# Attention and feed-forward on one core: 17-row score matmuls, an immediate exp bias, fuller PV groups, a reordered VectorE chain and a prologue without GpSimd fills

## The chip, the cores and the metric

The kernel runs on one core of one Trainium2 chip. The metric is the device time of one execution in microseconds (us); lower is better. Executions of one kernel are timed several times, beside executions of the kernel before on the same chip. A run is called slow when it lies over 1.5% above the fastest run of the same kernel; ratios use the others.

"Clock" always means the mean granted TensorE clock, as a share of full speed. It is a column of the profile.

## The reference

```python
def _A_ref(x, wqkv, wo):               # x [1, 2048, 512], H = 32 heads of Dh = 16
    q, k, v = split((x @ wqkv), 3, heads)
    scores = einsum("bhqd,bhkd->bhqk", q, k) * (Dh ** -0.5)
    p = softmax(scores)
    return merge(einsum("bhqk,bhkd->bhqd", p, v)) @ wo

def _B_ref(x, w1, w3, w2):             # F = 1792
    return (silu(x @ w1) * (x @ w3)) @ w2

xn = layernorm(x)
out = x + _A_ref(xn, wqkv, wo) + _B_ref(xn, w1, w3, w2)
```

This is abridged. Both blocks read the same normalized x, so the feed-forward work can fill TensorE's gaps in the attention. What matters here: 32 heads of only 16 dimensions, 2048 x 2048 scores for each head, all exponentiated.

## The kernel before

**The planner.** The order of the instructions on every engine is fixed when the kernel is built. A greedy planner simulates the engines with assumed costs (`dur=`), and at each step gives TensorE the first thing that can go: a score pair for ScalarE ("A"), a score pair for VectorE ("D"), a PV group, or a piece of a dense tile (K, Q, V, feed-forward, output).

**Scores.** Each of 1024 score pairs is two matmuls of 32 rows (the contraction) and 512 columns, on two of the four 32-row groups of the array; in the trace the two start 3 ns apart and are over in 0.39 us (medians at full clock). Only 16 rows are head dimensions. Row 16 of K and Q holds constants whose product adds a bias to each score. Rows 17 to 31 are zero. So the whole of KT and QT must be filled before K and Q are copied in, by ScalarE and GpSimd.

```python
def score(b0, name, dur):
    ...
    for i in range(2):
        j = j0 + i
        mms.append((b0 + i, KT[32 * j:32 * j + 32, g, kt * 128:(kt + 1) * 128],
                    QT[32 * j:32 * j + 32, u % 4, :], 32 * j))
    ...                                        # matmul(bank(b), l_, r_, tile_position=(rp, 0))

for g in range(2, NG):                         # prologue: six of these on GpSimd
    P.post("pool", lambda g=g: ... e.tensor_scalar(KT[:, g, :],
        sel1[:, 0:1].to_broadcast((128, S)), YB, None, ALU.mult) ..., ready=9.0 + g, prio=3)
```

**Exponentials.** ScalarE takes 798 of the pairs, with the bias in an SBUF column. VectorE takes 226, as a chain of five operations: clip to 16 bits (`yb`), mantissa (`mb`), exponent (`e`), correction (`g`), product (`t`).

```python
q = P.op("act", lambda e: e.activation(PT[:, s_, :], ps[:, b0 * 512:(b0 + 2) * 512], ACTF.Exp,
                                       scale=ASC, bias=act_bias[:, 0:1]), ..., dur=a_cost(1024))
...
for f_ in (f_m, f_e, f_g, f_t):                # e, g, t also write the shared keys XD
    P.post("dve", f_, ready=0.0, prio=2)
P.post("dve", p1, ready=o.end + _LAT, prio=3, cond=lambda: bool(slot()))
```

**PV.** Up to four matmuls of 128 rows and 17 columns stand side by side in the four 32-column groups, one for each of four heads, and run together: at 602.35 us of the trace four are over in 0.39 us, and one alone takes 0.38. A group that isn't full waits at most 1.2 us of planned time for its fellows.

```python
if len(pick) < 4 and not closed and P.t - oldest < 1.2:
    return False
...
ins = e.matmul(bank(PV)[32 * j:32 * j + 17, :], v_, p_, ..., tile_position=(0, 32 * j))
```

Dense tiles are cut the same way: four 32-column matmuls of 128 rows side by side.

## Time and profile before

| | before |
|---|---|
| time, median of the runs beside the change | 969.09 us (966.78 to 971.25) |
| prologue, 0 to 75 us | ScalarE 28.5 us busy, TensorE 44.1 |
| steady, 500 to 700 us | ScalarE 99%, VectorE 96%, TensorE 94% busy, clock 1.00 |
| tail, after the last exp | 43 us |

These lines are from the page of the kernel before: the span, the busy time of each engine (share of the span, number of instructions), the busy tenths and the clock tenths in 40 slices of the span, and the chain that ended last, by engine.

```profile
span 968.4 us, 21733 instructions
PE 858.6 (89%) x9033; PEld 240.4 (25%) x9033; DVE 878.7 (91%) x1437; ACT 853.9 (88%) x872; POOL 91.4 (9%) x82
...
PE   4669888989888999998989999999999999999985
...
DVE  7969797999899999999999999999999999999951
ACT  3339798999899999999999999999999999999930
...
PEclk9779799999989999999999999999999999999988
...
ACT 43%; DVE 33%; PE 17%; issue 2%; DMA 2%; SPq 2%; DVEq 0%
```

Three engines are near full for most of the span, and the chain lies mostly on the two that exponentiate. ScalarE is busy for only three tenths of the first three slices. Next, four groups of instructions: line, engine, operation, tiles, shapes and count; then busy us and mean ns of one; then the idle time before them and what ended it.

```profile
L1550 ACT ACTIVATE f_PT<-ps,f_act_bias 128x1024 bf16<-128x1024 f32 x798 | 819.1, 1153 | 51.3 <-PE ps L1513 44.1
L1513 PE MATMUL ps<-f_QT,f_KT 32*128 32x512 bf16 x2048 | 330.4, 391 | 42.4 <-ACT f_PT L1550 23.7
...
L1134 DVE TENSOR_SCALAR f_xn_sb<-f_xd,f_lnr,f_lnb 128x512 bf16<-128x512 bf16 x16 | 35.3, 2244 | 0.3 <-POOL f_lnb L1122 0.3
```

One of the 16 layer-norm scalings takes 2244 ns on average. The timelines of VectorE and of GpSimd show what the long ones run beside (start us, us, instruction):

```profile
26.82 10.83 DVE L1134 TENSOR_SCALAR f_xn_sb<-f_xd,f_lnr,f_lnb 128x512 bf16<-128x512 bf16 x2
```

```profile
26.77 10.73 POOL L1158 TENSOR_SCALAR f_KT<-f_sel 128x2048 bf16<-128x2048 f32 x2
```

Two scalings last as long as two GpSimd fills, within 0.1 us; two that run beside no fill, at 25.58 us, take 0.72 us. Last, the table of stretches: stretch, length, busy us (count) of PE, PEld, DVE, ACT and POOL, then the clock, the DMA share and GB/s.

```profile
0.00:75.00 75.00, 44.13 (x482) 17.00 (x482) 62.41 (x76) 28.51 (x32) 49.78 (x51) 0.84 0.37 100
75.00:300.00 225.00, 197.28 (x1898) 51.29 (x1890) 202.72 (x335) 204.93 (x208) 9.33 (x7) 0.94 0.23 31
500.00:700.00 200.00, 187.73 (x1994) 51.21 (x1994) 192.00 (x326) 198.51 (x204) 9.45 (x7) 1.00 0.25 29
927.00:968.00 41.00, 28.50 (x467) 12.35 (x463) 12.00 (x24) 1.79 (x3) 0.00 (x0) 0.86 0.21 37
```

### The profile page before, as it was taken

To read this page: it belongs to the slowest core of one execution; us is meant where nothing else is said; L and a number is where in the kernel's file an instruction comes from. 1 tells how busy PE (TensorE), PEld (TensorE's weight loads), DVE (VectorE), ACT (ScalarE), POOL (GpSimd) and SP (SyncE) were. 2 spreads that over 40 slices of the span, in tenths; PEclk is the share of its full clock that TensorE was granted. 3 is DMA by queue.
4 is the path that set the end of the run, shared out by engine and by line. 5 is a ranking of instruction groups with operands and counts; after the bars stand their busy time and mean duration, and the time that the engine had idled before them with its cause. 6 is when DMAs were issued, how large, how long until landed. Compare 5 with 4: busy or idle time off the path is not lost.

```text
span 968.4 us, 21733 instructions
## 1 busy us (share of the span) xinstructions
PE 858.6 (89%) x9033; PEld 240.4 (25%) x9033; DVE 878.7 (91%) x1437; ACT 853.9 (88%) x872; POOL 91.4 (9%) x82
## 2 busy tenths in 40 slices
PE   4669888989888999998989999999999999999985
PEld 2222122222222222222222222222222222222232
DVE  7969797999899999999999999999999999999951
ACT  3339798999899999999999999999999999999930
POOL 7840000000000000000000000000000000000000
PEclk9779799999989999999999999999999999999988
DMA  4501221312311222303232222222231212233221
GB/s 154 136 16 28 37 39 23 50 22 27 51 13 13 24 19 24 46 17 41 29 45 34 18 25 24 45 34 36 28 45 21 29 18 23 34 46 40 35 36 37
DMA packets 90685, 35.34 MB, mean 36 GB/s; under 512 B 74448, under 2 KB 88528, under 8 KB 90576
## 3 DMA queue, kind: packets, MB, share of 16 engines
q1 hardware_dynamic: 90576, 33.85, 24.7%
q8 instruction: 73, 1.20, 0.5%
q14 instruction: 36, 0.29, 0.1%
HBM read 22.81 MB, written 2.10 MB: 26 GB/s over the span
## 4 chain that ended last, share of the span: by engine, by line
ACT 43%; DVE 33%; PE 17%; issue 2%; DMA 2%; SPq 2%; DVEq 0%
ACT f_PT L1550 42%; DVE f_yb L1593 9%; PE ps L1216 8%; PE ps L1513 5%; DVE f_xd L1627 4%; PE ps L1673 4%; DVE f_xd L1610 3%; DVE f_xd L1621 3%; DVE f_mb L1616 3%; DVE f_xn_sb L1134 3%; DVE f_t L1350 2%; ACT f_th L1346 2%; SPq L1283 1%; DVE f_hT L1360 1%; DMA f_wkv<-in_A_wqkv_dram 1%
## 5 line engine op out<-in xcount | busy, mean ns | idle before, releaser
L1550 ACT ACTIVATE f_PT<-ps,f_act_bias 128x1024 bf16<-128x1024 f32 x798 | 819.1, 1153 | 51.3 <-PE ps L1513 44.1
L1513 PE MATMUL ps<-f_QT,f_KT 32*128 32x512 bf16 x2048 | 330.4, 391 | 42.4 <-ACT f_PT L1550 23.7
L1593 DVE TENSOR_SCALAR f_yb<-ps 128x1024 int16<-128x1024 f32 x226 | 274.4, 1214 | 5.3 <-PE ps L1513 4.9
L1673 PE MATMUL ps<-f_PT,f_Vaug 128*17 128x512 bf16 x1596 | 240.5, 389 | 4.5 <-DVE f_xd L1610 3.8
L1673 PE MATMUL ps<-f_xd,f_Vaug 128*17 128x512 bf16 x1356 | 238.7, 388 | 4.5 <-DVE f_xd L1610 2.9
L1216 PE MATMUL ps<-f_xnT,f_w 128*32 128x512 bf16 x1792 | 169.7, 396 | 19.4 <-DVE f_t L1350 13.8
L1513 PEld LDWEIGHTS ps<-f_QT,f_KT 32*128 32x128 bf16 x2048 | 83.0, 91 | 374.3 <-ACT f_PT L1550 291.8
L1627 DVE TENSOR_TENSOR f_xd<-f_yb,f_mb 128x1024 bf16<-128x1024 bf16 x226 | 159.5, 706 | 8.9
L1726 POOL TENSOR_TENSOR f_onorm<-f_U,f_R 128x512 bf16<-128x512 f32 x31 | 41.6, 1343 | 812.1 <-DMA f_R<-f_Rrow 532.3
L1616 DVE TENSOR_SCALAR f_mb<-f_yb 128x1024 int16<-128x1024 int16 x226 | 100.8, 446 | 5.1
L1621 DVE TENSOR_SCALAR f_xd<-f_yb 128x1024 int16<-128x1024 int16 x226 | 98.9, 438 | 7.1
L1610 DVE TENSOR_SCALAR f_xd<-f_yb 128x1024 int16<-128x1024 int16 x226 | 101.3, 448 | 0.0
L1673 PEld LDWEIGHTS ps<-f_PT,f_Vaug 128*17 128x17 bf16 x1596 | 55.4, 88 | 109.6 <-issue 83.0
L1216 PE MATMUL ps<-f_w,f_hT 128*32 128x512 bf16 x896 | 75.8, 381 | 0.5 <-DVE f_hT L1360 0.5
L1673 PEld LDWEIGHTS ps<-f_xd,f_Vaug 128*17 128x17 bf16 x1356 | 57.1, 89 | 69.6 <-issue 29.3
L1216 PEld LDWEIGHTS ps<-f_xnT,f_w 128*32 128x32 bf16 x1792 | 45.6, 96 | 70.2 <-issue 54.1
L1216 PE MATMUL ps<-f_wo,f_onorm 128*32 128x512 bf16 x512 | 46.0, 381 | 0.2 <-DVE f_wkv L1400 0.2
L1350 DVE SCALAR_TENSOR_TENSOR f_t<-f_th,ps 128x512 bf16<-128x512 f32 x56 | 38.1, 680 | 7.4 <-ACT f_th L1346 6.8
L1346 ACT ACTIVATE f_th<-ps 128x512 f32<-128x512 f32 x56 | 35.2, 629 | 10.6 <-PE ps L1216 10.6
L1360 DVE SCALAR_TENSOR_TENSOR f_hT<-f_t,ps 128x512 bf16<-128x512 bf16 x56 | 38.1, 681 | 4.1 <-PE ps L1216 2.6
L1134 DVE TENSOR_SCALAR f_xn_sb<-f_xd,f_lnr,f_lnb 128x512 bf16<-128x512 bf16 x16 | 35.3, 2244 | 0.3 <-POOL f_lnb L1122 0.3
L1216 PE MATMUL ps<-f_wkv,f_xnT 128*32 128x512 bf16 x256 | 24.4, 488 | 11.6 <-DVE f_t L1350 7.5
(54 smaller groups left out, 276.7 us busy)
## 6 DMA issues: line engine op xcount, KB each, us to landing
f_w<-in_B_w_dram SPq DMA_DIRECT2D x112, 128.0 KB, 2.8
f_R<-f_Rrow SPq DMA_DIRECT2D x128, 32.0 KB, 4.0
f_KT<-f_stg SPq DMA_DIRECT2D x128, 16.0 KB, 1.8
f_QT<-f_stg SPq DMA_DIRECT2D x128, 16.0 KB, 1.8
f_xr<-in_A_x_dram SPq DMA_DIRECT2D x16, 128.0 KB, 2.2
out_dram<-f_xn_sb SPq DMA_DIRECT2D x16, 128.0 KB, 1.9
f_w<-in_B_w_dram SPq DMA_DIRECT2D x1, 1792.0 KB
f_xd<-in_A_x_dram SPq DMA_DIRECT2D x3, 512.0 KB
```

Of the source, the lines that this page charges most:

```text
L1134: o = P.op("dve", lambda e: e.tensor_scalar(xn_sb[:, xs, :], x_sb[:, t, :], lnr[:, t:t + 1], lnb[:, t:t + 1], ALU.mult, ALU.add), reads=[( ...
L1216: ins = e.matmul(bank(bk)[32 * i:32 * i + 32, 0:ncols], make_lhsT(i), rhs_ap, start=start, stop=stop, tile_position=(0, 32 * i))
L1346: q = P.op("act", lambda e: e.activation(th[:, ss, :], bank(bk), ACTF.Tanh, scale=0.5), reads=[("ps", bk)], writes=[("th", ss)], dur=a_cos ...
L1350: q2 = P.op("dve", lambda e: e.scalar_tensor_tensor(t1[:, ss, :], th[:, ss, :], 1.0, bank(bk), ALU.add, ALU.mult), reads=[("th", ss), ("ps ...
L1513: ins = e.matmul(bank(b), l_, r_, start=True, stop=True, tile_position=(rp, 0))
L1550: q = P.op("act", lambda e: e.activation(PT[:, s_, :], ps[:, b0 * 512:(b0 + 2) * 512], ACTF.Exp, scale=ASC, bias=act_bias[:, 0:1]), reads= ...
L1593: q = P.op("dve", lambda e: e.tensor_scalar(yb[:, ys, :], ps[:, 4 * 512:6 * 512], 0.0, 32767.0, ALU.max, ALU.min), reads=[("ps", 4), ("ps" ...
L1610: q_ = P.op("dve", lambda e: e.tensor_scalar(dsl[:, s_, 0, :], yb[:, ys, :], 0x7F80, None, ALU.bitwise_and), reads=[("yb", ys)], writes=[( ...
L1616: P.op("dve", lambda e: e.tensor_scalar(mb[:, ys, :], yb[:, ys, :], 0x7F, 0x3F00, ALU.bitwise_and, ALU.bitwise_or), reads=[("yb", ys)], wr ...
L1621: q_ = P.op("dve", lambda e: e.tensor_scalar(dsl[:, s_, 1, :], yb[:, ys, :], -352.0, 0.0, ALU.add, ALU.max), reads=[("yb", ys)], writes=[( ...
L1627: q_ = P.op("dve", lambda e: e.tensor_tensor(dsl[:, s_, 2, :].bitcast(BF16), yb[:, ys, :].bitcast(BF16), mb[:, ys, :].bitcast(BF16), ALU.m ...
L1673: ins = e.matmul(bank(PV)[32 * j:32 * j + 17, :], v_, p_, start=s0, stop=s1, tile_position=(0, 32 * j))
```

## The change

The intent was to shorten each stage at once: a prologue without GpSimd's long fills, exps without the pointer operand, a VectorE chain without back-to-back dependences, and fewer TensorE slots by filling the PV groups. The score contraction goes from 32 rows to 17, which is what makes the fills unnecessary: rows 17 to 31 are no longer read. The planner's costs were re-fitted along with it, with a new surcharge of 0.1 us for each switch of TensorE between score matmuls and others.

The diff, cut to its core (cuts marked `...`):

```diff
-    P.op("act", ... QT ... KT fills from sel1 ...)       # ScalarE: QT and KT[0:2]
-    for g in range(2, NG): P.post("pool", ... KT[:, g, :] fill ...)
-    P.post("pool", late0, ...)                          # GpSimd: wo and R fills
+    e.memset(crow[:, 0, :], 1.0); e.memset(crow[:, 1, :], YB)          # on GpSimd, 4 x 512 each
+    P.dma(... QT[16:128:32, :, :] <- crow[:, 0, :] broadcast ...)
+    P.dma(... KT[16:128:32, :, :] <- crow[:, 1, :] broadcast ...)
+    P.op("act", fill(wo), ...); P.op("act", fill(R), ...); P.op("act", ... Vaug ones ...)
 ...
-    a_cost = lambda n: 0.113 + 0.000835 * n
-    d_cost = lambda n: 0.095 + 0.00104 * n
+    a_cost = lambda n: 0.10 + 0.000835 * n
+    d_cost = lambda n: 0.08 + 0.00104 * n
 ...
-    P.post("sp", late_loads, ready=20.0, prio=2, cond=lambda: "wo0" in done)
+    P.post("sp", late_loads, ready=20.0, prio=2)
 ...
-    DG = 0.24
+    DG = 0.23
+    mode = ["C"]
+    def pe_dur(m, d):
+        x = d + (0.1 if m != mode[0] else 0.0)
+        mode[0] = m
+        return x
 ...
-    mms.append((b0 + i, KT[32 * j:32 * j + 32, ...], QT[32 * j:32 * j + 32, ...], 32 * j))
+    mms.append((b0 + i, KT[32 * j:32 * j + 17, ...], QT[32 * j:32 * j + 17, ...], 32 * j))
 ...
-    o = P.op("pe", f, ..., dur=dur)                     # A 0.27; D 0.09 or 0.27
+    o = P.op("pe", f, ..., dur=pe_dur("S", dur))        # A 0.23; D 0.04 or 0.23
 ...
-    scale=ASC, bias=act_bias[:, 0:1]
+    scale=ASC, bias=A_BIAS
 ...
-    writes=[("ds", s_, 0)] + XD                          # also for g and t
+    writes=[("ds", s_, 0)] + xw                          # xw = XD if nd < ND else []
-    for f_ in (f_m, f_e, f_g, f_t): P.post("dve", f_, ready=0.0, prio=2)
-    P.post("dve", p1, ..., prio=3, cond=lambda: bool(slot()))
+    for f_, pr in ((f_m, 2), (f_e, 2), (f_g, 2), (f_t, 3)): P.post("dve", f_, ready=0.0, prio=pr)
+    P.post("dve", p1, ..., prio=2, cond=lambda: bool(slot()) and (nd < 2 or ("T", nd - 2) in done))
 ...
-    if len(pick) < 4 and not closed and P.t - oldest < 1.2:
+    if len(pick) < 4 and not closed and P.t - oldest < 3.0 and sum(f_ <= P.t for f_ in pr_free) > 1:
         return False
-    o = P.op("pe", f, ..., dur=0.25, name="pv%d" % u)
+    o = P.op("pe", f, ..., dur=pe_dur("C", 0.23), name="pv%d" % u)
```

Left out: other choices of PSUM banks in the prologue, all transposes evacuated on ScalarE, a third dense tile open at once in the prologue, and small corrections of the times assumed for VectorE.

## The prediction

> **What bounds the kernel now.** 1024 score pairs are exponentiated: 798 on ScalarE, 226 on VectorE (instruction groups). Three stages:

> - 0-75 us, prologue. ScalarE starts only 13 exps. VectorE's 16 layer-norm scalings take 35.3 us together, though one runs in 0.35 us when GpSimd is quiet. In the timeline they last 5.6, 10.8, 5.3 and 9.9 us exactly while GpSimd fills KT (5.37 us each, six of them). [...] TensorE starves, its granted clock 0.72-0.79.
> - 75-927 us, steady. Table of stretches, 500-700 us: ScalarE 99%, VectorE 96%, TensorE 94%. In 75-300 us ScalarE only 91% (TensorE clock 0.94). The chain of waits from 300 us is 55% exp.
> - 927-968 us, tail: 41 us after the last exp, mostly TensorE: unfinished FFN (8 us), about 20 us of output groups.

> **What changes, costed.**

> 1. Prologue. The GpSimd fills go away (two small DMAs and about 5 us of ScalarE fills in its idle time come instead). Scalings fall from 35 to about 6 us. VectorE work left is about 30 us after x arrives; loads finish about 23 us. The state of 75 us is reached at about 44: -30 us.
> 2. Immediate bias. Exps start every 1.005 us (nine in 9.05 us) and last 1.109 us alone; 512-column activations without a pointer are spaced 0.49. [...] I estimate 0.92 us spacing, 8% of the busiest engine.
> 3. VectorE chain. One pair takes 3.19 us start to start. From mask to subtract and from subtract to multiply, starts are 0.46 and 0.53 us apart instead of 0.34: same-engine dependencies, the first only because all three write the XD keys. The change drops XD after three pairs and puts the multiply behind the next pair's first ops. Estimate 2.9 us: -0.3 us x 226 = 66 us of VectorE.
> 4. Fuller PV groups. Two to four PV matmuls share one 0.215 us slot; the average is about three. Toward four saves about 7% of TensorE time. The 17-row contraction changes nothing: 512 columns stream anyway.
> 5. Tail. A freer TensorE does some FFN earlier: -6 us, uncertain.

> **On the critical path.** All three steady engines gain 7 to 9%, so the steady stage shortens. But the order is fixed at build time by assumed costs; ScalarE's assumed 0.955 us is slower than my 0.92, VectorE's assumed 2.82 faster than my 2.9, so VectorE (or TensorE) becomes the limit and ScalarE gets idle time. With T the steady length: (0.985T-30)/0.955 pairs on ScalarE plus (0.97T-115)/2.9 on VectorE must be 1010, T = 797; with today's costs the same sum gives 839 against 852 seen, so I use 805: -47 us.

> **Sum.** 44 + 805 + 35 = **884 us**, -9%. Range **853 to 912**. Faster by over 2%: 0.96; within 2%: 0.03; slower: 0.01.

> **What would show it.** No scaling above 0.8 us; ScalarE near full from 45 us; exp 1.02 us long, spaced about 0.92; chain 2.9 us; PV groups of four; in the steady stage VectorE busier than ScalarE (93-97%).

> **What would make it wrong.** Constant DMAs queued behind the loads, delaying the first scores; TensorE limiting at a lower clock; ds slots held longer by late multiplies and waiting PV groups; pointer cost already hidden by overlap (then about 915); unfinished FFN lengthening the tail.

Three passages are cut out of points "0-75 us" and 2, where marked: they rested on figures and a mechanism that no trace of this case shows. The 0.92 us in point 2 was the author's estimate. The trace of the kernel before gives the same estimate: ScalarE's activations without a pointer take 0.60 us for 512 columns and 1.89 us for 2048, so 0.43 us for 512 more; with the 0.49 us between two of 512 columns this makes 0.92.

## More of the kernel before

An assumed cost changes no instruction, but it changes the order.

In the steady stage TensorE runs at full clock and is still 94% busy.

## The result, and the profile after

The kernel after takes 1250.71 us (median of four runs, 1237.0 to 1261.67), beside 969.09 us before. The ratio is 1.28, with a 95% interval of 1.2715 to 1.2885. Ratios here are the mean time of one kernel's fast runs over that of the other's of the same rounds, so not quite the ratio of the medians quoted. The prediction was 884 us, 9% faster; the kernel became 28% slower.

The page of the kernel after, the same lines as before:

```profile
span 1235.1 us, 21867 instructions
PE 1155.8 (94%) x9033; PEld 233.0 (19%) x9033; DVE 829.9 (67%) x1434; ACT 843.2 (68%) x874; POOL 53.5 (4%) x72
...
PE   4799999999999999999999999998999999989656
...
DVE  5368776677766997766777655689876766657322
ACT  4578777677776997777777666689877776647210
...
PEclk9666555555555995555555555579655555575588
...
PE 84%; DVE 8%; DMA 4%; SPq 1%; issue 1%; ACT 1%; POOL 0%; DVEq 0%; POOLq 0%
```

The same number of matmuls (9033) takes 1156 us of TensorE instead of 859. The clock row explains it: 5 in most slices, where before it was 9. TensorE is the limit, at 84% of the chain, and ScalarE and VectorE, which were to be relieved, are idle a third of the time. The groups of the kernel after (the last from the first 75 us alone):

```profile
L1543 ACT ACTIVATE f_PT<-ps 128x1024 bf16<-128x1024 f32 x798 | 798.8, 1027 | 298.8 <-PE ps L1509 258.7
L1509 PE MATMUL ps<-f_QT,f_KT 17*128 17x512 bf16 x2048 | 452.9, 563 | 17.8 <-DMA f_KT<-f_stg 7.4
```

```profile
L1134 DVE TENSOR_SCALAR f_xn_sb<-f_xd,f_lnr,f_lnb 128x512 bf16<-128x512 bf16 x16 | 6.0, 409 | 10.4 <-PE ps L1233 8.8 <-POOL f_lnb L1121 1.6
```

The local savings are all there: an exp fell from 1153 to 1027 ns, the scalings from 35.3 to 6.0 us. But one score matmul went from 391 to 563 ns, and ScalarE waits 299 us for the scores. The stretches of the kernel after, and three windows of 3.4 us:

```profile
0.00:75.00 75.00, 51.62 (x506) 17.23 (x506) 31.65 (x70) 40.79 (x45) 11.92 (x41) 0.77 0.38 98
75.00:300.00 225.00, 222.13 (x1560) 39.79 (x1556) 166.25 (x281) 167.49 (x171) 8.04 (x6) 0.53 0.20 26
500.00:700.00 200.00, 199.20 (x1362) 33.74 (x1361) 143.90 (x248) 149.01 (x154) 8.00 (x6) 0.50 0.17 21
1150.00:1235.00 85.00, 50.09 (x699) 19.82 (x691) 21.73 (x37) 6.67 (x11) 0.00 (x0) 0.76 0.20 39
303.40:306.80 3.40, 3.40 (x30) 0.46 (x22) 1.02 (x2) 2.43 (x3) 0.00 (x0) 0.50 0.06 10
...
402.80:406.20 3.40, 3.37 (x50) 0.93 (x38) 3.40 (x6) 3.40 (x5) 0.00 (x0) 1.00 0.17 48
```

From 500 to 700 us TensorE is busy for 199.2 of 200 us and is granted half the clock throughout. In the two short windows it is busy all the time in both; in one the clock is 0.50 and 30 matmuls are run, in the other 1.00 and 50. So a busy TensorE is not what keeps its clock up. The tail, too, is longer: 85 us after the last exp instead of 43.

The clock record itself is finer than these tables. For the kernels before and after it holds two values alone, 0.5 and 1.0, and its 19 and 21 changes all fall on a grid of 3.413 us, within 3 ns. So the short windows above are about one step of it.

### The profile page after: what moved, and what is told of

The parts are those of the page before. It is cut to its first block, busy times and chain, and to the rows that moved or that the text cites. A ratio compares the mean times of both kernels' runs of the same rounds, so it can differ in the third digit from the quotient of the medians.

```text
span 1235.1 us, 21867 instructions
## 1 busy us (share of the span) xinstructions
PE 1155.8 (94%) x9033; PEld 233.0 (19%) x9033; DVE 829.9 (67%) x1434; ACT 843.2 (68%) x874; POOL 53.5 (4%) x72
## 4 chain that ended last, share of the span: by engine, by line
PE 84%; DVE 8%; DMA 4%; SPq 1%; issue 1%; ACT 1%; POOL 0%; DVEq 0%; POOLq 0%
PE ps L1509 29%; PE ps L1204 29%; PE ps L1670 26%; DVE f_yb L1587 3%; DMA f_w<-in_B_w_dram 2%; DMA f_KT<-f_stg 1%; DVE f_xd L1621 1%; DVE f_mb L1610 1%; DVE f_xd L1604 1%; DMA f_wkv<-in_A_wqkv_dram 1%; DVE f_xd L1615 1%; ACT f_PT L1543 1%; SPq L1279 0%; PE ps L1233 0%; DVE f_hT L1356 0%
## 5 line engine op out<-in xcount | busy, mean ns | idle before, releaser
L1543 ACT ACTIVATE f_PT<-ps 128x1024 bf16<-128x1024 f32 x798 | 798.8, 1027 | 298.8 <-PE ps L1509 258.7
L1509 PE MATMUL ps<-f_QT,f_KT 17*128 17x512 bf16 x2048 | 452.9, 563 | 17.8 <-DMA f_KT<-f_stg 7.4
L1670 PE MATMUL ps<-f_PT,f_Vaug 128*17 128x512 bf16 x1596 | 331.7, 562 | 7.3 <-DVE f_xd L1604 5.3
L1670 PE MATMUL ps<-f_xd,f_Vaug 128*17 128x512 bf16 x1356 | 303.9, 570 | 2.9 <-DVE f_xd L1621 2.2
L1204 PE MATMUL ps<-f_xnT,f_w 128*32 128x512 bf16 x1792 | 230.7, 576 | 26.2 <-DMA f_w<-in_B_w_dram 23.7
L1509 PEld LDWEIGHTS ps<-f_QT,f_KT 17*128 17x128 bf16 x2048 | 84.7, 98 | 546.3 <-issue 341.4
L1204 PE MATMUL ps<-f_w,f_hT 128*32 128x512 bf16 x896 | 97.8, 509 | 2.3 <-DVE f_hT L1356 1.3
L1670 PEld LDWEIGHTS ps<-f_xd,f_Vaug 128*17 128x17 bf16 x1356 | 49.7, 95 | 88.5 <-issue 53.1
L1687 DVE COPY f_U<-ps 128x512 f32<-128x512 f32 x32 | 22.0, 689 | 33.4 <-PE ps L1670 28.4
L1204 PE MATMUL ps<-f_xnT,f_wq 128*32 128x512 bf16 x256 | 34.6, 575 | 0.3 <-DVE f_hT L1356 0.3
```

What stands on the lines that cost most here:

```text
L1204: ins = e.matmul(bank(bk)[32 * i:32 * i + 32, 0:ncols], make_lhsT(i), rhs_ap, start=start, stop=stop, tile_position=(0, 32 * i))
L1509: ins = e.matmul(bank(b), l_, r_, start=True, stop=True, tile_position=(rp, 0))
L1670: ins = e.matmul(bank(PV)[32 * j:32 * j + 17, :], v_, p_, start=s0, stop=s1, tile_position=(0, 32 * j))
```

## The experiments

There were two questions. What halves the clock: the rows of the scores, the columns, TensorE's idle time, or the order? And what else in the change costs or saves time? Theory 1: the clock follows how many of the 128 array rows are driven, so 17 rows instead of 32 lower it. Rivals: the clock follows how many cells (rows times columns) are used; the clock follows idle gaps, and the change's order makes more of them; and the loss comes from the planner's new order, with the clock a consequence. The expectations use letters. R is theory 1. C counts cells. S blames the order. T and M are two forms of theory 1 for matmuls that stand side by side: T counts the time in which rows are driven, M adds up the rows of every matmul.

Eighteen kernels ran. All gave correct results. Unless said otherwise the time is a median of all runs, with its range; ratios use the fast runs alone. Fast runs of the kernel before in these batches had medians of 970 to 972 us. A ratio within 2% of 1 counts as the same, so the gains below 2% in what follows are small ones.

### b_k17: the kernel before with 17-row scores and nothing else

```diff
-                mms.append((b0 + i, KT[32 * j:32 * j + 32, g, kt * 128:(kt + 1) * 128],
-                            QT[32 * j:32 * j + 32, u % 4, :], 32 * j))
+                mms.append((b0 + i, KT[32 * j:32 * j + 17, g, kt * 128:(kt + 1) * 128],
+                            QT[32 * j:32 * j + 17, u % 4, :], 32 * j))
```

Theory R's own words are cut from this text; R is theory 1, as above.

> The kernel before with one edit: score matmuls contract 17 rows instead of 32 (rows 17 to 31 hold zeros, so the arithmetic is the same). Theory R [...]: granted clock 0.5 to 0.7, over 1150 us. Rival S (the new schedule, its prologue and its fuller PV groups cost the clock, the rows do not matter): clock 0.96, 960 to 975 us as before.

Measured: 1044.53 us (1004.72 to 1082.77, five runs), ratio 1.0429 (1.0341 to 1.0517; two fast runs, 1004.72 and 1018.35). The clock was 0.82 to 0.90, against about 0.96 before. The direction is that of theory R, but its numbers (clock 0.5 to 0.7, over 1150 us) were missed: this kernel gets back to full clock more often than was thought. The profile is of the slowest run. In its stretch from 300 to 500 us:

```profile
300.00:500.00 200.00, 198.22 (x1336) 37.14 (x1332) 131.05 (x215) 141.98 (x134) 6.38 (x5) 0.55 0.15 17
```

This is the picture of the kernel after: TensorE 99% busy at about half the clock. The order is that of the kernel before to the last instruction; no slot was saved or added. So the rows alone cost clock. The runs spread by 8%, and the time goes with the clock: 1004.72 us at 0.898, 1082.77 at 0.82.

### b_k24: the same with 24 rows

```diff
-                ... KT[32 * j:32 * j + 32, ...], QT[32 * j:32 * j + 32, ...]
+                ... KT[32 * j:32 * j + 24, ...], QT[32 * j:32 * j + 24, ...]
```

> The kernel before with 24 score rows, half way of the dose. Theory R with a graded count: between, the half clock sets in but can be left again, clock 0.65 to 0.95, 980 to 1200 us. If the count goes by whole 32-row blocks (and b_k17 is then slow for another reason): 968 us. Rival S: 968 us.

Measured: 981.51 us (975.86 to 989.02), ratio 1.0128 (1.0062 to 1.0193), clock 0.927 to 0.945. Eight rows fewer cost 1.3%, fifteen cost 4.3%: the effect is graded, and it is not that 17 is an odd size. The 1.3% is within the 2% that counts as the same; the lower clock is the clearer sign.

### a_k32: the kernel after with 32-row scores

KT and QT have to be zero where the constants are not, so this adds nine zero fills on VectorE.

```diff
+        P.op("dve", lambda e: e.memset(QT[:, :, :]..., 0.0), ...)
+        def zfill(g):
+            P.op("dve", lambda e: e.memset(KT[:, g, :].bitcast(FP32), 0.0), ...)
+        ...                                    # constants of KT by DMA after the fills, by pairs of g
-                mms.append((b0 + i, KT[32 * j:32 * j + 17, ...], QT[32 * j:32 * j + 17, ...], 32 * j))
+                mms.append((b0 + i, KT[32 * j:32 * j + 32, ...], QT[32 * j:32 * j + 32, ...], 32 * j))
```

> The changed kernel with 32-row score matmuls again; KT and QT are zero filled by VectorE, the rest of the change is kept. Theory R: clock above 0.93, 860 to 910 us, and the gain that was predicted appears. Rival S: clock stays near 0.6, over 1150 us.

Measured: 1016.57 us (1014.02 to 1029.27), ratio to before 1.0476 (1.0445 to 1.0507), clock 0.896 to 0.909. Fifteen rows of zeros take 225 us off the kernel after (fast runs: 1015.7 against 1240.4 us), although the fills are added. But it stays 5% above the kernel before, where theory 1 alone expected it well below. So something else in the change costs time as well.

### a_pv32: the kernel after with 32-column PV matmuls

```diff
-                    ins = e.matmul(bank(PV)[32 * j:32 * j + 17, :], v_, p_, ...)
+                    ins = e.matmul(bank(PV)[32 * j:32 * j + 32, :], v_, p_, ...)     # V padded by its neighbour
```

> The changed kernel with 17-row scores, but PV matmuls of 32 output columns instead of 17 (the extra columns are never used). Theory R in the form that only rows count: clock about 0.6, 1200 to 1270 us, no cure. Theory C (rows times columns, cells of the array): the added columns give back more activity than the 15 rows took, clock above 0.93, 850 to 910 us. Rival S: no cure.

Measured: 1264.9 us (1256.86 to 1289.24), ratio 1.3019, clock 0.556 to 0.584. Nearly twice as many columns of the array take part in each PV matmul, and the clock does not rise. Counting cells instead of rows is ruled out.

### b_bias, b_pv4, b_chain: one part of the change each, on the kernel before

b_bias, the immediate bias alone:

```diff
-                                                       scale=ASC, bias=act_bias[:, 0:1]),
+                                                       scale=ASC, bias=-127.0 * math.log(2.0) + math.log(KAPPA)),
```

> The kernel before with the exp bias as an immediate and nothing else; the order of instructions on TensorE and VectorE is the same. If the pointer costs spacing as predicted: exps 1.02 us long and 0.92 apart, ScalarE no longer the limit, 935 to 960 us, clock 0.96 or higher. If the cost was hidden: 965 to 972 us. If a ScalarE that waits more lowers the clock: slower than 972 us.

Measured: 964.23 us (959.27 to 966.84), ratio 0.9921 (0.9878 to 0.9964). An exp alone is 1.02 us long; where ScalarE runs without a stop, 15 take 14.51 us, so they start (14.51 - 1.02)/14 = 0.96 us apart. From 300 to 900 us:

```profile
300.00:900.00 600.00, 565.20 (x6018) 154.55 (x6014) 579.87 (x971) 567.50 (x610) 30.49 (x23) 0.99 0.25 31
```

ScalarE is no longer the fullest engine; VectorE is, at 97%. The saving of the busiest engine is worth only what the next one leaves: 0.8%, less than the recorded 935 to 960 us.

b_pv4, the fuller PV groups alone:

```diff
-            if len(pick) < 4 and not closed and P.t - oldest < 1.2:
+            if len(pick) < 4 and not closed and P.t - oldest < 3.0 and \
+                    sum(f_ <= P.t for f_ in pr_free) > 1:
```

The condition of theory T is cut from this text: the first numbers are T's, the second M's.

> The kernel before with only the fuller PV rule (planned PV groups fall from 1049 to 778; the same 2952 PV matmuls, 32-row scores). [...] less of it, clock clearly below 0.96, 0.85 to 0.93, and 990 us or more. If it counts every matmul's rows (theory M): clock 0.96 and 940 to 970 us.

Measured: 989.22 us (981.22 to 990.33), ratio 1.0165 (1.0112 to 1.0218), clock 0.897 to 0.910. The trace counts 778 PV groups instead of 1049, so the rule does what it says, and saves a quarter of the PV slots. The kernel becomes slower by 1.7%, which at a limit of 2% is unclear, and the clock falls, which is clear. That the time is lost through the clock, and not through PV matmuls that wait longer for their fellows, is argued here and not shown.

b_chain, the VectorE chain alone:

```diff
+            xw = XD if nd < ND else []
-                              reads=[("yb", ys)], writes=[("ds", s_, 0)] + XD, dur=0.34)
+                              reads=[("yb", ys)], writes=[("ds", s_, 0)] + xw, dur=0.34)
 ...                                                       # g and t likewise
-                for f_ in (f_m, f_e, f_g, f_t):
-                    P.post("dve", f_, ready=0.0, prio=2)
-            P.post("dve", p1, ready=o.end + _LAT, prio=3, cond=lambda: bool(slot()))
+                for f_, pr in ((f_m, 2), (f_e, 2), (f_g, 2), (f_t, 3)):
+                    P.post("dve", f_, ready=0.0, prio=pr)
+            P.post("dve", p1, ready=o.end + _LAT, prio=2,
+                   cond=lambda: bool(slot()) and (nd < 2 or ("T", nd - 2) in done))
```

> The kernel before with only the reordered VectorE chain and without the XD keys after the third pair (planned PV groups 873). VectorE start to start 2.9 instead of 3.19 us in full stretches. With ScalarE still the limit: 950 to 970 us at clock 0.96 by theory M; by theory T the fewer PV groups lower the clock a little, 0.92 to 0.95, 970 to 1000 us.

Measured: 967.32 us (966.21 to 968.98), ratio 0.9966 (0.9938 to 0.9994), clock 0.936 to 0.946. VectorE is relieved (from 300 to 900 us 559.6 us busy, before 575.3), but ScalarE with its pointer is still the limit (585.4 us, before 592.1). The clock is that of theory T, the time that of theory M.

### b_bias_chain: both together

The edit is that of b_bias and that of b_chain.

> The kernel before with the immediate bias and the VectorE chain together, nothing else. b_bias alone gained 0.8% and left VectorE at 97%, b_chain alone gained 0.3% with ScalarE the limit. If each hid the other's gain: 920 to 950 us. If the clock takes the gain away (theory T: planned PV groups 873 instead of 1049): clock 0.93 to 0.95 and 950 to 968 us.

Measured: 954.78 us (948.98 to 956.12, five runs), ratio 0.984 (0.9818 to 0.9863), clock 0.933 to 0.952. The two are worth 1.6% together, more than the 0.8% and 0.3% of each, because each removes the limit that the other runs into. This version beats both kernels, if the one before by less than 2%.

### b_pv4_zero: does the clock follow driven rows? Useless work as a test

To the kernel of b_pv4, in the same order, a matmul with zero weights and 128 rows is added to most full PV groups (660 of them in the trace). It changes no result.

```diff
+                if len(mms) == 4 and go:
+                    j, v_, p_ = go[0][:3]
+                    e.matmul(bank(PV)[32 * j:32 * j + 17, :], zpad[:, :], p_, start=False, stop=False,
+                             tile_position=(0, 32 * j))
```

> b_pv4 with the same order of instructions, but each PV group of four gets one useless matmul of zero weights that adds 0 to the PV bank: about 690 slots of 0.215 us with all 128 rows driven. Theory T (the clock follows the time in which array rows are driven): clock back from 0.90 to 0.95 or more, and in spite of 148 us of added TensorE work no slower than b_pv4, 965 to 990 us. If the clock follows useful work or column count, or not activity at all: clock 0.90 or lower and over 1020 us.

Measured: 1021.25 us (1017.91 to 1024.59), ratio 1.0514 (1.0476 to 1.0553), clock 0.968 to 0.977. The time missed the expectation: each useless matmul costs a slot, and this is more than the clock gives back. The clock is what the test was for. From 500 to 700 us, b_pv4 and then b_pv4_zero:

```profile
500.00:700.00 200.00, 179.20 (x1950) 47.15 (x1942) 183.15 (x304) 193.84 (x199) 11.20 (x8) 0.93 0.26 33
```

```profile
500.00:700.00 200.00, 185.34 (x1972) 55.05 (x1964) 174.19 (x285) 187.13 (x184) 9.29 (x7) 1.00 0.23 28
```

Work that does nothing raised the clock from 0.93 to 1.00. The order of the useful work is the same, so the order does not set the clock.

### a_k32_late_oldpv: two suspects for the 5% that a_k32 has left

The old PV rule, and the 1.8 MB load of w2 moved from 20 to 60 us, on a_k32.

```diff
+        P.post("sp", w2_load, ready=60.0, prio=2)
-            if len(pick) < 4 and not closed and P.t - oldest < 3.0 and sum(...) > 1:
+            if len(pick) < 4 and not closed and P.t - oldest < 1.2:
```

> The changed kernel with 32-row scores, the old PV rule (planned groups 849 instead of 776) and the 1.8 MB load of w2 moved behind the prologue. Theory T: clock 0.92 to 0.96 against 0.90 of a_k32. The K rows no longer wait 11 us behind w2. 900 to 980 us; theory M expects the clock of a_k32 (0.90) outside the prologue and 980 to 1010 us.

Measured: 1023.93 us (1020.96 to 1033.62), ratio 1.0559, clock 0.902 to 0.920. A miss: neither helps. But its last exp starts at 945.6 us, and 79 us follow, with 696 dense matmuls left over. In the kernel before, 43 us and 464 follow. The 5% is in the tail.

### a_k32_pecost and a_k32_late_pecost_oldpv: the planner's old costs for TensorE

```diff
-        DG = 0.23
+        DG = 0.24
-            x = d + (0.1 if m != mode[0] else 0.0)
+            x = d
-            x = score(2 * buf, "A", 0.23)
+            x = score(2 * buf, "A", 0.27)
-            x = score(4, "D", 0.04 if mode[0] == "S" else 0.23)
+            x = score(4, "D", 0.09 if st["lastA"] + 0.05 > P.t else 0.27)
-            o = P.op("pe", f, ..., dur=pe_dur("C", 0.23), ...)       # PV
+            o = P.op("pe", f, ..., dur=pe_dur("C", 0.25), ...)
```

> a_k32 with the old TensorE costs in the planner (no 0.1 us for a switch between score and other matmuls). With the switch cost the planner lets dense tiles starve: 684 dense matmuls came after the last exp, against 464 before, and the tail grew from 43 to 85 us. With the old costs the plan leaves 7 tiles: tail 25 to 35 us, last exp no later than 945 us, 950 to 980 us in all, clock 0.91 to 0.95. If the tail is long for another reason it stays near 85 us and the time near 1017.

Measured: 954.59 us (953.49 to 959.83), ratio 0.9848 (0.9811 to 0.9885), clock 0.923 to 0.937. The tail is 28 us, with 312 dense matmuls in it. Assumed costs, which are in no instruction, were worth 61 us (fast runs: 1015.7 to 954.6), nearly all of it in the tail (85.2 us in a_k32). From 300 to 900 us:

```profile
300.00:900.00 600.00, 543.86 (x6056) 147.54 (x6054) 556.34 (x956) 557.51 (x604) 31.05 (x23) 0.96 0.26 32
```

No engine is full any more; each waits for another for about 7% of the time or more.

a_k32_late_pecost_oldpv makes the same edit on a_k32_late_oldpv.

> As a_k32_pecost, with the old PV rule and w2 loaded later. Theory T: more PV groups (861 planned against 774) keep the clock higher, 0.94 to 0.97, and this is 10 to 30 us faster than a_k32_pecost: 925 to 960 us, so faster than both kernels. If the PV rule does not matter for the clock here: the same as a_k32_pecost within 1%.

Measured: 958.95 us (956.8 to 961.67), ratio 0.9878 (0.9846 to 0.9909), clock 0.937 to 0.942, tail 33 us. The costs matter in the same way here; the late load and the old PV rule make no gain on top.

### a_pecost: the old costs with 17 rows

The edit is that of a_k32_pecost, on the kernel after itself.

> The changed kernel with 17-row scores and only the old TensorE costs in the planner. If the planner's starved dense tiles were what let the clock fall: clock over 0.9, 940 to 1000 us. If the 17 rows are enough by themselves in the changed schedule (theory T): clock 0.55 to 0.75, 1080 to 1230 us.

Measured: 1142.79 us (1126.36 to 1160.41), ratio 1.1666 (1.1574 to 1.1757), clock 0.649 to 0.674, tail 31 us. This completes a square for the changed kernel, of medians of the fast runs (two runs in each cell of the upper row, four in the lower):

| us | new planner costs | old planner costs |
|---|---|---|
| 17 rows | 1240.4 | 1131.6 |
| 32 rows | 1015.7 | 954.6 |

Rows alone, at old costs: 177 us. Costs alone, at 32 rows: 61 us. Both: 286 us, more than the sum.

### b_newcost: the new costs on the kernel before

```diff
+        def pe_dur(m, d): ...                  # 0.1 us for each switch, as in the change
-            x = score(2 * buf, "A", 0.27)      # and D, PV, DG likewise
+            x = score(2 * buf, "A", 0.23)
```

> The kernel before with only the changed kernel's TensorE costs in the planner (0.1 us for each switch between score and other matmuls). If these costs are what starves the dense tiles: 650 to 720 dense matmuls after the last exp instead of 464, a tail of 70 to 90 us instead of 43, clock 0.93 to 0.97, 995 to 1030 us. If the long tail came from another part of the change: 43 us and 965 to 975 us.

Measured: 1046.82 us (1039.54 to 1050.99), ratio 1.0765 (1.0717 to 1.0813). The clock is 0.93 to 0.945, a little lower. The last exp starts at 964.3 us (before: 925.3) and 85.0 us follow (before: 43.1), with 704 dense matmuls left. The tail is as expected; the time is above the expected 1030 us, because the stretch before the last exp is 39 us longer too. What lengthens that stretch was not looked into. The chain in that tail (start us, us, what):

```profile
974.15 2.51 DMA f_w<-in_B_w_dram
976.66 0.04 issue
976.70 3.21 PE ps L1216 x28
979.97 0.38 SPq L1198
...
1012.05 25.86 PE ps L1216 x444
```

With the surcharge the planner gives TensorE less to do before the last exp, and dense tiles, which have the lowest priority, are left over. The surcharge itself isn't wrong: at full clock in the kernel before, score pairs and column-tiled groups that alternate start 0.32 us apart (medians, both ways), and a group after a group 0.22 us. The new costs come to 0.33 us for a score pair or a PV group after a switch, the old ones to 0.27 and 0.25. So the truer costs gave the worse order; why this greedy planner does better with the smaller ones is not shown. At the end each left-over pair of feed-forward tiles waits for its own load of weights (2.5 us) and then runs 3.2 us, one after another. The kernel after has the same tail: 85.4 us, 684 left.

### a_fill, a_k32_pecost_fill, b_bias_chain_fill: can useless work be put where the array is idle?

A score pair leaves two of the four row groups idle. These kernels put zero-weight matmuls there (17 rows in a_fill, 32 in the others), into the PV bank.

```diff
+                for (jj, r_) in extra:         # the two row groups the score pair does not use
+                    e.matmul(bank(PV)[32 * jj:32 * jj + 17, :], zpad[32 * jj:32 * jj + 17, :], r_, start=False,
+                             stop=False, tile_position=(32 * jj, 32 * jj))
```

> The changed kernel with its 17-row scores and its plan, but 894 of the 1024 score pairs get two useless 17-row matmuls of zero weights in the two row groups that the pair leaves idle (they add 0 to the PV bank). They should run beside the pair, in its slot. Theory T (rows driven, over time): the score slots drive 68 rows instead of 34, slightly more than the 64 of 32-row scores, so the clock comes back to about 0.9 as in a_k32 and the time to 990 to 1050 us. If only the rows of useful data or the columns count, or the fill takes its own time: clock 0.6, over 1200 us.

> a_k32_pecost with the same fill of 32 rows each: score slots drive all 128 rows instead of 64. Theory T: clock from 0.93 to 0.97 or more; if the clock is what keeps a_k32_pecost from the predicted 884 us, 905 to 940 us; if in-order waits keep it, 945 to 960 us at a clock of 0.98.

> b_bias_chain with the fill of 32 rows. Theory T: clock from 0.95 to 0.98 and 925 to 945 us against 955. If the fill costs TensorE time of its own: slower than 960 us.

Measured: a_fill 1822.57 us (1780.87 to 1843.58, clock 0.532 to 0.559), a_k32_pecost_fill 1190.08 (1160.96 to 1226.38), b_bias_chain_fill 1208.97 (1199.29 to 1210.01). Against the kernels they were made from they all lost a quarter to a half. The fill does not run beside the score pair, as the TensorE timeline of a_k32_pecost_fill shows:

```profile
603.94 0.38 PE L1540 MATMUL ps<-f_QT,f_zpad 32*17 32x512 bf16 x2
604.25 0.39 PE L1543 MATMUL ps<-f_QT,f_KT 32*128 32x512 bf16 x2
604.59 0.38 PE L1540 MATMUL ps<-f_QT,f_zpad 32*17 32x512 bf16 x2
```

Each starts some 0.32 us after the one before. Two score pairs that use all four row groups do run together: four score matmuls are over in 0.40 us at 602.02 us of the kernel before. The fill has tiles of 32 columns, the score tiles of 128. Whether that is the reason is not shown: no kernel with fills as wide as the scores' is among the runs. As tests of the clock the fills are clean. From 600 to 1000 us, a_fill and a_k32_pecost_fill:

```profile
600.00:1000.00 400.00, 399.45 (x2348) 70.54 (x2344) 196.96 (x338) 206.10 (x209) 10.61 (x8) 0.54 0.13 16
```

```profile
600.00:1000.00 400.00, 396.65 (x3858) 107.23 (x3856) 292.67 (x494) 300.70 (x309) 16.57 (x12) 0.97 0.20 24
```

Two kernels with a TensorE busy for over 99% of the time, one at clock 0.54 and one at 0.97. Scores and fills drive 17 rows in the first, 32 in the second.

### b_bias_chain_pv4: what the new prologue is worth

The edits of b_bias, b_chain and b_pv4 together, on the old prologue. Beside a_k32_pecost this leaves mainly the prologue as a difference.

> The kernel before with immediate bias, VectorE chain and fuller PV groups, but its old prologue, 32 rows and planner costs; it differs from a_k32_pecost by the prologue (and 0.013 us in the planner's cost of an exp). Against b_bias_chain (955 us, clock 0.95) theory T expects the fuller groups to cost clock: 0.91 to 0.94 and 955 to 985 us. If the prologue is worth the predicted 30 us: about 985 us against 955 for a_k32_pecost; if only about 5 us as the pairs done at 100 us say: 955 to 965.

Measured: 987.47 us (984.7 to 998.0), ratio 1.0211 (1.0145 to 1.0277), clock 0.888 to 0.912. Read naively, the new prologue saves 33 us. But at 100 us the two kernels are only six pairs apart (43 and 49 pairs begun, some 5 us of work), and at 300 us 31 (238 and 269). Between 100 and 300 us VectorE of b_bias_chain_pv4 waits 31 us at three places for the row sums, with them in a queue behind other DMAs; in a_k32_pecost 11.5 us. The longest, on VectorE and on the queue that issues DMAs:

```profile
112.18 0.25 DVE L1712 RECIPROCAL f_Rc<-f_Lc 128x16 f32<-128x16 f32 x1 [11.34 <-DMA f_Lc<-f_U]
```

```profile
98.94 6.14 SPq L1283 DMA_DIRECT2D f_KT<-f_stg  x9
105.12 5.03 SPq L1283 DMA_DIRECT2D f_QT<-f_stg  x8
110.25 0.69 SPq L1700 DMA_DIRECT2D f_Lc<-f_U  x1
```

The sums are issued after 17 small DMAs that each hold the queue for some 0.65 us. That is luck of order, not worth of the prologue. What the prologue alone is worth is not settled by this run.

## The rule that the traces show

With all the traces at hand, one more thing could be counted. The clock record changes only on the grid of 3.413 us. For each such window I added up the rows that its TensorE slots drive, and looked at the clock of the next window. A score matmul counts its rows (17, 24 or 32), a group of column-tiled matmuls counts 128 once, and a transpose of 128 columns counts a quarter of 128. A slot of 512 columns takes about 0.21 us at full clock, so a window holds 16; the sum over 16 is the mean number of driven rows. In all 20 traces (before, after and the 18 experiments) there are 6,223 windows:

| driven rows in a window | windows | next window at half clock |
|---|---|---|
| under 44 | 1405 | 1390 |
| 44 to 52 | 932 | 574 |
| 52 and more | 3886 | 14 |

It also shows why the kernel after does not get out of half clock again. The last column takes the windows at half clock in which TensorE was over 97% busy, and tells how many of them were followed by full clock:

| kernel | drops to half clock | windows at half clock | of the busy ones, full clock next |
|---|---|---|---|
| before (32 rows, 1049 PV groups) | 9 | 19 of 276 | 7 of 9 |
| b_k24 | 10 | 34 of 279 | 10 of 23 |
| b_k17 | 14 | 112 of 309 | 12 of 101 |
| b_pv4 (32 rows, 778 groups) | 18 | 54 of 281 | 17 of 26 |
| a_pecost (17 rows, 772 groups) | 11 | 222 of 329 | 11 of 198 |
| after (17 rows, 776 groups) | 10 | 291 of 354 | 8 of 271 |

The kernel before drops to half clock nine times and the kernel after ten. One window with too few rows was enough: in a recount of its trace, at each drop of the kernel before the last window at full clock held under 47 rows, the one ahead of it 45 to 92. A TensorE of that kernel that catches up at half clock drives over 50 rows (median) and mostly gets full clock back at the next window (7 of 9). In the kernel after it drives 41 to 44 (medians of the two counts), below 48, though it has no idle time left. It stays there, some 29 windows for each drop (291/10), until the mix of work happens to hold enough of the wide slots: in the recount the window before each return to full clock held 47 to 64 rows.

## Why the prediction was wrong, point by point

**The step that failed** is in point 4: "The 17-row contraction changes nothing: 512 columns stream anyway." The columns do stream in the same time at the same clock: a score matmul lasts 384 ns in the kernel before and 385 ns in the kernel after at full clock, 602 and 603 ns at half clock (medians). But the clock followed the rows. At old planner costs this is worth 177 us on the changed kernel (a_pecost against a_k32_pecost) and 4.3% on the kernel before (b_k17). With it fell "All three steady engines gain 7 to 9%, so the steady stage shortens": TensorE was costed at the clock of before, 0.99 from 300 to 900 us, and got 0.60 there. The text did list "TensorE limiting at a lower clock" among the ways to be wrong, but gave slower a chance of one in a hundred.

**Fuller PV groups** were to save "about 7% of TensorE time". The slots were saved (776 groups for 1049), and b_pv4 shows the price: with fewer slots that drive 128 rows its clock fell to 0.90, and b_pv4_zero got the clock back by adding such slots. b_pv4 lost 1.7%, so on the kernel before the saving was at best nothing. On the changed kernel the old rule was no better: 958.95 us in a_k32_late_pecost_oldpv, 954.59 in a_k32_pecost.

**The tail** was to be 6 us shorter; it is 42 us longer (85.4 against 43.1). The cause is the planner's new costs for TensorE, as b_newcost shows on the kernel before (+42 us of tail, +7.65% in all) and a_k32_pecost on the changed one (28 us of tail with the old costs). The prediction costed instructions and passed over the numbers in the diff that are no instruction.

**Immediate bias: right in mechanism, worth less than was said.** An exp is 1027 ns long and starts 0.93 us (in a full-clock stretch of the kernel after, 15 in 14.09 us) to 0.96 us (b_bias) after the one before; predicted were 1.02 and 0.92. An exp alone took 1109 ns with the pointer (before) and 1020 ns without (b_bias), 89 ns less. It was worth 0.8% alone, since VectorE became the limit at once.

**VectorE chain: right.** A pair took 3.19 us start to start before (3.12 is the median of 37 pairs with nothing between) and 2.93 (three pairs in 8.79 us) to 3.07 us in a full-clock stretch after; predicted were 2.9. Worth 0.3% alone, 1.6% with the bias.

**Prologue: mechanism right, size not shown.** No scaling is above 0.42 us any more, and the long waits beside GpSimd's fills are gone. Before, two scalings took 10.83 us beside 10.73 us of fills, and 0.72 us beside none; why VectorE takes so long beside them is not in the trace. But "-30 us" did not come. The kernel after has begun 49 pairs at 100 us where the kernel before has begun 43, about 5 us of work. Other waits stepped in. The longest stands in its chain:

```profile
34.13 11.15 DMA f_KT<-f_stg
```

K rows land 11 us after the first of them was issued, where such a copy of 16 KB mostly takes 1.8 us (median of 128). Just ahead of them in the queue, 0.55 us before, stands the w2 load of 1.8 MB, which no longer waits for the GpSimd fills, and the issues of eight such copies hold the queue for 9.11 us. How much of the wait is due to either is not shown. Loading w2 later brought nothing: at 100 us a_k32_late_pecost_oldpv, with the old PV rule too, has begun 48 pairs where a_k32_pecost has 49. The clock may be a part (0.77 in the first 75 us, 0.84 before). The cause stays open.

**What stays open.** Without the two faults the changed kernel takes 955 us, not 884. Nothing is full there (93% each for ScalarE and VectorE, clock 0.93 to 0.96). The small DMAs that hold their queue and the waits in fixed order may be a part of it (VectorE waits 11.5 us for row sums between 100 and 300 us), and so may the nine zero fills that the 32-row form adds. How the missing 70 us are split between these, the clock and the prologue has not been measured.

The best versions are a_k32_pecost (954.59 us, ratio 0.985) and b_bias_chain (954.78 us, ratio 0.984). The second is the simpler: the kernel before with an immediate bias and the new VectorE chain.

## What to carry to other kernels

Before you thin out TensorE's work (fewer rows in a contraction, fewer and fuller groups), look at what its clock hangs on: a TensorE that is full but drives few rows can be held at half speed (here 199.2 of 200 us busy at clock 0.50), and then a small saving can cost more than it brings (here 28%, where 9% was to be gained). Look at the granted clock first whenever a matmul count stays the same and its busy time rises. In a kernel whose order is planned from assumed costs, treat a changed cost as a change of the program, and try each part of a bundle alone on the old kernel before you add up savings.
